# Elementwise work of stage 1 and of the weight conversions, done on VectorE instead of GpSimd

## The chip, the core and the metric

The kernel runs on one core of a Trainium2 chip. A core has five engines, each with an instruction queue of its own that is worked through in order: TensorE (PE, matrix products into PSUM), VectorE (DVE), ScalarE (ACT), GpSimd (POOL), and SyncE (SP), which here issues all DMAs. They wait for each other by semaphores. The metric is the device time of one execution in microseconds, lower is better; three executions of the kernel before gave 1600.19, 1600.63 and 1602.12.

## The reference

The attention is a double one: 32 "pack" vectors per head attend to the keys and values, and the queries attend to the result. Two feed-forward layers follow, each with its own nonlinearity.

```python
def _attn_ref(q, k, v, p):                     # 8 batches, 8 heads, 576 positions, 64 wide
    scale = 1.0 / np.sqrt(q.shape[-1])
    def sm_attn(qq, kk, vv):
        s = scale * np.matmul(qq, kk.transpose(0, 1, 3, 2))
        s = s - np.max(s, axis=-1, keepdims=True)
        a = np.exp(s)
        a = a / (np.sum(a, axis=-1, keepdims=True) + 1e-09)
        return np.matmul(a, vv)
    p_packed = sm_attn(p, k, v)                # 32 rows per head
    return sm_attn(q, p_packed, p_packed)

def _moe_ref(x, w_in, w_out):                  # 4608 tokens, 512 -> 2048 -> 512
    h = x @ w_in
    return (h - np.tanh(h)) @ w_out

def _moe2_ref(x, w_in, w_out):
    h = x @ w_in
    return (h * np.cos(h)) @ w_out
```

The weights arrive as 64-bit floats, seen by the kernel as pairs of 32-bit words.

## The kernel before

**Split numbers.** Products are wanted at float32 precision from matmuls on rounded operands (`F32R`). So an operand is kept as a high half (the value rounded by a ScalarE copy) and a low half (the value minus the high half), and a product is three matmuls: high by high, low by high, high by low. Making a low half is one elementwise subtraction: L359 for attention weights `a2`, L167 for weights `w1o`, `w2i`, `w2o`, L485 and L608 for the nonlinearities' results `gl`, L553 for the second layer's input `yhl`.

**Weight conversions (class `Conv`).** A tile of 128x512 64-bit weights (`st`) is loaded; then three parts, which the program places by tables. `a`: ScalarE scales the high words (L121). `b`: VectorE shifts the result left by 3 (L133, `shift`), merges the sign bit (L138, `sign`) and merges three bits from the low words (L143, `low`). `c`: ScalarE rounds the finished tile into the high half (L166) and the low half is subtracted (L167, on POOL). For 23 of the 32 tiles of the first layer (`POOL_SIGN`) the sign is done otherwise: ScalarE makes a tile of signs (L123), POOL multiplies by it (L148), and `sign` is left out. Tiles of `w1i` have no part `c`.

**Stage 1: attention and the first layer.** The tokens are 16 blocks of 288 (`blk`), two per batch. A step (128 in all, numbered n) takes two of the 16 slices of the hidden layer: `h1` multiplies the attention weights by `gw` (the packed values times `w_in`, made by `gmat`, split by `gsplit`), 12 matmuls; `el1` and `el2` compute h - tanh(h) with five VectorE instructions (L465 `t`, L466 `d`, L485 `gl` of the step before, L468 `y`, L472 copy_predicated into `y`); `ymm1`, 24 matmuls, follows two steps later. PSUM tiles for `h` and for all attention products share two buffers. The attention of batch b runs beside the steps of batch b-1 (functions put into `early[n]` and `mid[n]`): its second softmax is `s2m` (maximum, subtraction L336), `s2e`, `s2n` (sum, multiplication L348), `s2t`, `s2h` (split, L359). For b > 0 the three elementwise operations run on POOL; for b = 0 only the split does.

**What sets the order.** Everything ahead of step 15 is ordered by the scheduler of the kernel language, from then on the queues have the order in which the code issues. In a step the conversion's VectorE operations (`fill`) are put between the five instructions of `el2` by `interleave`. Steps 112 to 127 convert the second layer's weights, one tile per step; the rest is converted in `el_cos` of token block t = 0 of stage 2, three tiles per step.

**Stage 2: the second layer.** The tokens are nine blocks of 512 (t), with eight steps s each: `h2` (24 matmuls), `el_cos`, `ymm2` (24 matmuls) one step later. `el_cos` is a chain: ACT adds a constant (L586), DVE L589, ACT Sin and Square (L595, L596), DVE L599, ACT rounds `gh` (L605), DVE subtracts `gl` (L608). Between its links stand the calls `each("ca")` and `each("b")`, one conversion part each. The POOL split L553 of the next block's input stands in steps 2 to 5.

Of the kernel before, what the change touches and what calls it, by code (L numbers as in the profile page):

```python
# [10 lines left out]
F32 = mybir.dt.float32  # L11
# [4 lines left out]
AF = mybir.ActivationFunctionType  # L16
ALU = mybir.AluOpType
# [13 lines left out]
    "i2 i0 i3 i1 o1 o0 i4 i5 i6 i7 o3 o4 o2 o5 o7 i8 "  # L31
    "o6 i9 i10 i11 i14 o9 i12 i13 o8 i15 o11 o13 o12 o10 o15 o14"
).split()
POOL_SIGN = "11111111111111101011100010111000"
PRE_A = (0, 1, 1, 1, 1, 0, 1, 1, 1, 0, 1, 1, 0, 0, 0)
PRE_B = (1, 0, 1, 1, 2, 0, 2, 2, 0, 1, 2, 2, 0, 3, 0)
STEP_A = (1, 2, 2, 2, 1, 2, 1, 1, 1, 1, 0, 2, 1, 1, 1, 1, 1, 1, 0, 3, 1, 1)
# [13 lines left out]
def fused_kernel(ctx, tc, qT, kT, v, pT, w1i, w1o, w2i, w2o, ident, out):  # L51
    nc = tc.nc
    B, _, _, _, HB = qT.shape
# [13 lines left out]
    wp = ctx.enter_context(tc.tile_pool(name="wp", bufs=32))  # L67
# [7 lines left out]
    def f32(ap):  # L75
        return ap.bitcast(F32)

    def wtile(name):
        return wp.tile([128, 2, 512], F32R, tag="w", name=name)
# [7 lines left out]
    class Conv:  # L87
# [19 lines left out]
        def a(self):  # L107
            self.prefetch()
            if not self.ready:
                return  # L110
            kind, f, st = self.ready.pop(0)
            tmp, sgn = self.alloc_tmp(self.na, kind)
            self.na += 1
            w = tmp
            if kind == "w1i":
                if f // 2 not in w1in:
                    w1in[f // 2] = wp.tile([128, 2, 512], F32, tag="w", name="w1i")
                w = w1in[f // 2][:, f % 2, :]
            sv = st.rearrange("p (n two) -> p n two", two=2)
            hi, lo = sv[:, :, 1], sv[:, :, 0]  # L120
            nc.scalar.activation(out=w, in_=f32(hi), func=AF.Copy, scale=2.0 ** -112)  # L121
            if sgn is not None:
                nc.scalar.activation(out=sgn, in_=f32(hi), func=AF.Sign)  # L123
            self.done_a.append((kind, f, hi, lo, w, sgn))

        def b_ops(self):
            if not self.done_a:
                return []
            kind, f, hi, lo, w, sgn = self.done_a.pop(0)
            wi = w.bitcast(I32)  # L130

            def shift():
                nc.vector.tensor_scalar(  # L133
                    out=wi, in0=wi, scalar1=3, scalar2=None, op0=ALU.logical_shift_left
                )

            def sign():
                nc.vector.scalar_tensor_tensor(  # L138
                    out=wi, in0=hi, scalar=SGN, in1=wi, op0=ALU.bitwise_and, op1=ALU.bitwise_or
                )  # L140

            def low():
                nc.vector.scalar_tensor_tensor(  # L143
                    out=wi, in0=lo, scalar=29, in1=wi,
                    op0=ALU.logical_shift_right, op1=ALU.bitwise_or,
                )
                if sgn is not None:
                    nc.gpsimd.tensor_tensor(out=w, in0=w, in1=sgn, op=ALU.mult)  # L148
                if kind == "w1i":
                    self.bdone.add(f)  # L150
                else:
                    self.done_b.append((kind, f, w))
                self.prefetch()

            return [shift, low] if sgn is not None else [shift, sign, low]

        def b(self):
            for fn in self.b_ops():
                fn()

        def c(self):
            if not self.done_b:
                return
            kind, f, w = self.done_b.pop(0)
            t = wtile(kind)
            nc.scalar.activation(out=t[:, 0, :], in_=w, func=AF.Copy)  # L166
            nc.gpsimd.tensor_tensor(out=t[:, 1, :], in0=w, in1=f32(t[:, 0, :]), op=ALU.subtract)  # L167
            {"w1o": w1out, "w2i": w2in, "w2o": w2out}[kind][f] = t

        def c_all(self):  # L170
            while self.done_b:
                self.c()

        def need_i(self, f):
            while f not in self.bdone:
# [21 lines left out]
    def zip_ops(lists):  # L197
        out = []
        for i in range(0, len(lists), 2):
            pair = lists[i:i + 2]  # L200
            for j in range(max(len(p) for p in pair)):
                out += [p[j] for p in pair if j < len(p)]
        return out
# [51 lines left out]

    def attention(b, half, at=None, tsc=0, ttr=0, tpp=0, ts2=0):
        x = {}
        eng = nc.vector if b == 0 else nc.gpsimd

        def sc():  # L260
            k = ld.pop(("k", b, half))
# [71 lines left out]
        def s2m():  # L333
            m = att.tile([128, NG], F32, tag="m", name="m")
            nc.vector.tensor_reduce(out=m, in_=x["u3"], axis=AX.X, op=ALU.max)
            eng.tensor_tensor(  # L336
                out=x["u3"], in0=x["u3"], in1=m.to_broadcast([128, NG, 32]), op=ALU.subtract
            )

# [3 lines left out]
        def s2n():  # L343
            r = att.tile([128, NG], F32, tag="r", name="r")
            nc.vector.tensor_reduce(out=r, in_=x["u3"], axis=AX.X, op=ALU.add)
            nc.vector.tensor_scalar(out=r, in0=r, scalar1=1e-9, scalar2=None, op0=ALU.add)
            nc.vector.reciprocal(out=r, in_=r)
            eng.tensor_tensor(  # L348
                out=x["u3"], in0=x["u3"], in1=r.to_broadcast([128, NG, 32]), op=ALU.mult
            )  # L350

# [4 lines left out]
        def s2h():  # L356
            t = a2p.tile([128, 2, S], F32R, tag="a2", bufs=4, name="a2")
            nc.scalar.activation(out=t[:, 0, :], in_=x["ut"], func=AF.Copy)
            nc.gpsimd.tensor_tensor(  # L359
                out=t[:, 1, :], in0=x["ut"], in1=f32(t[:, 0, :]), op=ALU.subtract  # L360
            )
            a2[b, half] = t
# [66 lines left out]
    def h1(blk, s, st):  # L429
        b, j = divmod(blk, 2)  # L430
        h = pss("h")
        for x in range(2):
            f = 2 * s + x
            c0 = 128 * (f % 4)
            n = 0
            for ga, aa in ((0, 0), (1, 0), (0, 1)):
                for half in range(2):
                    nc.tensor.matmul(  # L438
                        out=h[:, x, 0:HB],
                        lhsT=gw[b, f // 4, half][:, ga, c0:c0 + 128],  # L440
                        rhs=a2[b, half][:, aa, HB * j:HB * j + HB],
                        start=(n == 0), stop=(n == 5),
                    )
                    n += 1
        st["h"] = h[:, :, 0:HB]
# [201 lines left out]
    def run_pool(name, **kw):  # L647
        c = tc.tile_pool(name=name, bufs=1, reuse_waits="tile", **kw)
        return c, c.__enter__()
# [14 lines left out]
        return wp.tile([128, 1024], I32, tag="w", name="st")  # L664

    def alloc_tmp(i, kind):
        t = wp.tile([128, 2, 512], F32, tag="w", name="wt")
        return t[:, 0, :], (t[:, 1, :] if POOL_SIGN[i] == "1" else None)

    conv = Conv([("w1" + o[0], int(o[1:])) for o in ORDER], 3, alloc_st, alloc_tmp)  # L670

# [100 lines left out]
    p2x = {}  # L772

    def open_p2r():
        attc.__exit__(None, None, None)
        cstc.__exit__(None, None, None)
        p2x["c"], p2x["r"] = run_pool("p2r", side="right")
        p2x["conv"] = Conv(
            todo2, 3,
            lambda i: p2x["r"].tile([128, 1024], I32, tag="st", bufs=3, name="st"),  # L780
            lambda i, kind: (p2x["r"].tile([128, 512], F32, tag="wt", bufs=2, name="wt"), None),
        )

    for n in range(-16, 0):
# [8 lines left out]
    for n, (blk, s) in enumerate(steps):  # L793
        if n == NSTEP * (NB - 2):
            open_p2r()
            p2r, conv2 = p2x["r"], p2x["conv"]
        if n == STEP_ORDERED:
            sched.__exit__(None, None, None)
            sched = tc.manual_schedule()
            sched.__enter__()  # L800
        st = {}
        h1(blk, s, st)
        el1(st)
        cv = conv2 if blk >= NB - 2 else conv
        cv.c_all()
        for fn in early[n]:
            fn()
        if hist:
            el3(hist[-1][2])
        if blk >= NB - 2:  # L810
            na = STEP_A2[n - NSTEP * (NB - 2)]
        else:
            na = STEP_A[n] if n < len(STEP_A) else 1
        fill = zip_ops([cv.b_ops() for _ in range(len(cv.done_a))])
        if n < 32:
            for _ in range(na):
                cv.a()
        el2(st, hist[-1][2] if hist else None, fill)
        if blk >= NB - 2:
            for _ in range(na):  # L820
                cv.a()
        if n == Y2LOAD:
            yr0 += [loady(0, k) for k in range(2)]
        if n == Y2SPLIT:
            yt = [splity(0, yr0.pop(0), nc.gpsimd) for k in range(2)]
            yr0 += [loady(0, k) for k in range(2, 4)]
        for fn in mid[n]:
            fn()
        hist.append((blk, s, st))
        if len(hist) == 3:  # L830
            hb, hs, hst = hist.pop(0)
            ymm1(hb, hs, hst)
            if hb < NP and hs == HS - 1:
                ypart1(hb)
            if hs == NSTEP - 1:
                yevac1(hb)
# [84 lines left out]
```

## Time and profile before

| | |
|---|---|
| median of 3 runs | 1600.63 us (1600.19 to 1602.12) |
| the profiled execution | 1600.74 us, its span 1599.0 us |
| PE busy | 1523.6 us, 95% |
| DVE busy | 1011.8 us, 63% |
| ACT busy | 871.4 us, 54% |
| POOL busy | 218.1 us, 14% |

The span is the time from the first to the last instruction of the profiled execution. Of POOL's time 60.1 us are the 34 splits L553, which the change leaves where they are. The engines' shares over the whole span say little here, as the program runs through stages with different loads: stage 1 ends at about 802 us, and beside its first 180 us and its last 90 us weights are converted. Rows of the trace give start and length of an instruction; a length in the order-of-time view runs until its end, and the next instruction of the same engine can start a little before.

### The profile page before, as it was taken

What the parts mean: (1) busy time and instruction counts of PE and PEld (TensorE: products, weight loads), DVE (VectorE), ACT (ScalarE), POOL (GpSimd) and SP (SyncE); (2) the same over time, 40 slices, a digit from 0 to 9 for tenths busy, and PEclk for the clock granted to TensorE, in tenths of its full rate; (3) what the DMA queues carried; (4) which work ended last, traced back from release to release, by engine and by line L of the source; (5) the groups of instructions that cost most, each with busy time, mean ns of one, the idle gap of its engine ahead of it and who ended that gap; (6) DMA issues with size and microseconds to landing.
All of it is one profiled execution on the core that took longest, in us unless ns stands there. A gap on an engine that the chain in (4) does not pass through costs nothing.

```text
span 1599.0 us, 25218 instructions
## 1 busy us (share of the span) xinstructions
PE 1523.6 (95%) x10336; PEld 1321.6 (83%) x10336; DVE 1011.8 (63%) x1357; ACT 871.4 (54%) x1331; POOL 218.1 (14%) x154
## 2 busy tenths in 40 slices
PE   3789999999999999997898999999999999999999
PEld 1678888999999999997877788888888888888887
DVE  6999888787878788789979433333333333333333
ACT  4768665665666566676666444444444443444443
POOL 3633110100101010111224010100001010101000
PEclk6799999999999999999999999999999999999999
DMA  9423222211211121022334101001010101010000
GB/s 347 147 100 119 78 79 90 64 46 34 76 36 58 60 64 60 31 80 95 94 114 139 40 14 40 14 1 53 0 47 7 42 12 40 14 40 14 23 4 27
DMA packets 49138, 97.63 MB, mean 61 GB/s; under 512 B 4928, under 2 KB 26432, under 8 KB 49024
## 3 DMA queue, kind: packets, MB, share of 16 engines
q1 hardware_dynamic: 49024, 96.03, 18.2%
q8 instruction: 81, 1.33, 0.4%
q14 instruction: 33, 0.27, 0.1%
HBM read 74.78 MB, written 21.23 MB: 60 GB/s over the span
## 4 chain that ended last, share of the span: by engine, by line
PE 78%; DVE 13%; issue 4%; ACT 2%; DMA 2%; SPq 0%; POOL 0%; DVEq 0%; ACTq 0%; POOLq 0%
PE y L625 22%; PE h L564 22%; PE y L500 20%; PE h L438 10%; DVE wt L133 2%; DVE y L468 2%; DVE wt L143 2%; PE gp L400 2%; DVE wt L138 2%; DVE d L466 1%; DVE t L465 1%; DVE y L472 1%; DVE gl L485 1%; ACT wt L121 1%; PE sc L250 1%
## 5 line engine op out<-in xcount | busy, mean ns | idle before, releaser
L564 PE MATMUL h<-yhl,w2i 128*128 128x512 f32 x1728 | 403.2, 389 | 0.0
L564 PEld LDWEIGHTS h<-yhl,w2i 128*128 128x128 f32 x1728 | 324.4, 188 | 67.1
L500 PE MATMUL y<-gh,w1o 128*128 128x288 f32 x2048 | 311.3, 304 | 16.8 <-ACT gh L480 11.8
L500 PEld LDWEIGHTS y<-gh,w1o 128*128 128x128 f32 x2048 | 284.1, 191 | 45.9 <-ACT t L453 14.9
L625 PE MATMUL y<-w2o,gh 128*128 128x512 f32 x1152 | 274.6, 390 | 7.4 <-ACT gh L605 7.4
L625 PEld LDWEIGHTS y<-w2o,gh 128*128 128x128 f32 x1152 | 215.7, 188 | 55.2 <-ACT gh L605 10.9
L589 DVE SCALAR_TENSOR_TENSOR a<-a,h 128x1024 f32<-128x1024 f32 (+1 forms) x74 | 88.0, 1192 | 244.9 <-ACT a L586 244.9
L438 PE MATMUL h<-a,g 128*128 128x288 f32 x1536 | 230.5, 300 | 12.8 <-ACT w1i L121 6.6
L438 PEld LDWEIGHTS h<-a,g 128*128 128x128 f32 x1536 | 214.9, 192 | 17.0 <-ACT w1i L121 7.5
L586 ACT ACTIVATE a<-h 128x1024 f32<-128x1024 f32 (+1 forms) x74 | 74.1, 1005 | 243.1 <-PE h L564 241.6
L453 ACT ACTIVATE t<-h 128x576 f32<-128x576 f32 x128 | 83.2, 650 | 207.6 <-PE h L438 207.3
L599 DVE SCALAR_TENSOR_TENSOR a<-a,h 128x1024 f32<-128x1024 f32 (+1 forms) x74 | 88.1, 1192 | 143.3 <-ACT a L596 143.3
L500 PE MATMUL y<-gl,w1o 128*128 128x288 f32 x1024 | 160.0, 299 | 1.2 <-DVE gl L485 1.2
L500 PEld LDWEIGHTS y<-gl,w1o 128*128 128x128 f32 x1024 | 145.0, 191 | 1.5 <-DVE gl L485 1.4
L625 PE MATMUL y<-w2o,gl 128*128 128x512 f32 x576 | 142.8, 390 | 0.0
L553 POOL TENSOR_TENSOR yhl<-yr,yhl 128x512 fp32r<-128x512 f32 x34 | 60.1, 1768 | 549.6 <-ACT yhl L552 549.6
L608 DVE TENSOR_TENSOR gl<-a,gh 128x1024 fp32r<-128x1024 f32 (+1 forms) x74 | 88.4, 1196 | 73.3 <-ACT gh L605 73.2
L465 DVE TENSOR_TENSOR t<-h,t 128x576 f32<-128x576 f32 x128 | 95.3, 744 | 52.8 <-ACT u L454 52.5
L625 PEld LDWEIGHTS y<-w2o,gl 128*128 128x128 f32 x576 | 108.2, 188 | 22.5 <-DVE gl L608 0.2
L472 DVE COPY_PREDICATED y<-k,t 128x576 f32<-128x576 int16 x128 | 118.4, 925 | 11.6
L595 ACT ACTIVATE a<-a 128x1024 f32<-128x1024 f32 (+1 forms) x74 | 76.7, 1037 | 83.3 <-DVE a L589 83.3
L605 ACT ACTIVATE gh<-a 128x1024 fp32r<-128x1024 f32 (+1 forms) x74 | 76.6, 1036 | 83.1 <-DVE a L599 83.1
(79 smaller groups left out, 1541.8 us busy)
## 6 DMA issues: line engine op xcount, KB each, us to landing
y<-ye SPq DMA_DIRECT2D x80, 144.0 KB, 1.9
yr<-y SPq DMA_DIRECT2D x36, 256.0 KB, 3.5
out<-o SPq DMA_DIRECT2D x36, 256.0 KB, 2.1
st<-w1i SPq DMA_DIRECT2D x16, 512.0 KB, 7.4
v<-vv SPq DMA_DIRECT2D x16, 512.0 KB, 4.5
st<-w1o SPq DMA_DIRECT2D x16, 512.0 KB, 6.5
st<-w2i SPq DMA_DIRECT2D x16, 512.0 KB, 3.6
st<-w2o SPq DMA_DIRECT2D x16, 512.0 KB, 3.6
```

What stands on the lines that cost most here:

```text
L438: nc.tensor.matmul(out=h[:, x, 0:HB], lhsT=gw[b, f // 4, half][:, ga, c0:c0 + 128], rhs=a2[b, half][:, aa, HB * j:HB * j + HB], start=(n = ...
L453: nc.scalar.activation(out=st["t"], in_=h, func=AF.Tanh)
L465: lambda: nc.vector.tensor_tensor(out=t, in0=hs, in1=t, op=ALU.subtract),
L472: lambda: nc.vector.copy_predicated(out=y, mask=k.bitcast(I16), data=t),
L500: nc.tensor.matmul(out=yps[blk][d][:, 0:HB], lhsT=w1out[f][:, wh, 128 * d:128 * d + 128], rhs=st[gg][:, x, :], start=(s in first and x == ...
L564: nc.tensor.matmul(out=h[:, x, :], lhsT=w2in[f][:, wa, 128 * k:128 * k + 128], rhs=yt[k][:, ya, :], start=(n == 0), stop=(n == 11),)
L589: nc.vector.scalar_tensor_tensor(out=a[:, x], in0=a[:, x], scalar=MAGIC, in1=h[:, x], op0=ALU.subtract, op1=ALU.subtract,)
L595: nc.scalar.activation(out=a[:, x], in_=a[:, x], func=AF.Sin, scale=PI)
L599: nc.vector.scalar_tensor_tensor(out=a[:, x], in0=a[:, x], scalar=1.0, in1=h[:, x], op0=ALU.subtract, op1=ALU.mult,)
L605: nc.scalar.activation(out=gh[:, x], in_=a[:, x], func=AF.Copy)
L608: nc.vector.tensor_tensor(out=gl[:, x], in0=a[:, x], in1=f32(gh[:, x]), op=ALU.subtract)
L625: nc.tensor.matmul(out=yps[t][m], lhsT=st[gg][:, x, 128 * m:128 * m + 128], rhs=w2out[f][:, wh, :], start=(s == 0 and x == 0 and part == 0 ...
```

## The change

The three attention operations (L336, L348, L359) go to VectorE for every batch. `POOL_SIGN` and its sign tiles go: all tiles take `shift`, `sign`, `low`, and the 23 ScalarE sign passes and 23 POOL multiplications are gone. The low half in `c` goes to VectorE. Called from a step of stage 1, `c_all` collects these subtractions and hands them back, and the step puts them at the head of `fill`, that is, between the instructions of `el2`. Called from `el_cos` or from `need`, `c` issues the subtraction at once.

```diff
-            tmp, sgn = self.alloc_tmp(self.na, kind)
+            tmp = self.alloc_tmp(self.na, kind)
...
             nc.scalar.activation(out=w, in_=f32(hi), func=AF.Copy, scale=2.0 ** -112)
-            if sgn is not None:
-                nc.scalar.activation(out=sgn, in_=f32(hi), func=AF.Sign)
...
-                if sgn is not None:
-                    nc.gpsimd.tensor_tensor(out=w, in0=w, in1=sgn, op=ALU.mult)
...
-            return [shift, low] if sgn is not None else [shift, sign, low]
+            return [shift, sign, low]
...
-        def c(self):
+        def c(self, later=None):
...
             nc.scalar.activation(out=t[:, 0, :], in_=w, func=AF.Copy)
-            nc.gpsimd.tensor_tensor(out=t[:, 1, :], in0=w, in1=f32(t[:, 0, :]), op=ALU.subtract)
+            rest = lambda: nc.vector.tensor_tensor(
+                out=t[:, 1, :], in0=w, in1=f32(t[:, 0, :]), op=ALU.subtract
+            )
+            rest() if later is None else later.append(rest)
...
         def c_all(self):
+            later = []
             while self.done_b:
-                self.c()
+                self.c(later)
+            return later
...
-        eng = nc.vector if b == 0 else nc.gpsimd
...
-            eng.tensor_tensor(
+            nc.vector.tensor_tensor(
                 out=x["u3"], in0=x["u3"], in1=m.to_broadcast([128, NG, 32]), op=ALU.subtract
...
-            eng.tensor_tensor(
+            nc.vector.tensor_tensor(
                 out=x["u3"], in0=x["u3"], in1=r.to_broadcast([128, NG, 32]), op=ALU.mult
...
-            nc.gpsimd.tensor_tensor(
+            nc.vector.tensor_tensor(
                 out=t[:, 1, :], in0=x["ut"], in1=f32(t[:, 0, :]), op=ALU.subtract
...
-        cv.c_all()
+        rest = cv.c_all()
...
-        fill = zip_ops([cv.b_ops() for _ in range(len(cv.done_a))])
+        fill = rest + zip_ops([cv.b_ops() for _ in range(len(cv.done_a))])
```

The new file is two lines shorter, so its line numbers are lower by one to five: L464 there is L465 here (`t`), L130 is L133 (`shift`), L135 is L138 (`sign`), L140 is L143 (`low`), L162 is L167 (the low half), L588, L598 and L607 are L589, L599 and L608.

First excerpt: VectorE's queue over one of the steps 114 to 125 of stage 1, before, from `t` to the copy_predicated.

```order
L465 TENSOR_TENSOR t<-h,t 128x576
L133 TENSOR_SCALAR wt<-wt 128x512
L466 TENSOR_TENSOR d<-u,h 128x576
L138 SCALAR_TENSOR_TENSOR wt<-st,wt 128x512
L485 TENSOR_TENSOR gl<-y,gh 128x576
L143 SCALAR_TENSOR_TENSOR wt<-st,wt 128x512
L468 SCALAR_TENSOR_TENSOR y<-y,d 128x576
L472 COPY_PREDICATED y<-k,t 128x576
```

The same engine and step in the changed kernel.

```order
L464 TENSOR_TENSOR t<-h,t 128x576
L162 TENSOR_TENSOR w2i<-wt,w2i 128x512
L465 TENSOR_TENSOR d<-u,h 128x576
L130 TENSOR_SCALAR wt<-wt 128x512
L484 TENSOR_TENSOR gl<-y,gh 128x576
L135 SCALAR_TENSOR_TENSOR wt<-st,wt 128x512
L467 SCALAR_TENSOR_TENSOR y<-y,d 128x576
L140 SCALAR_TENSOR_TENSOR wt<-st,wt 128x512
L471 COPY_PREDICATED y<-k,t 128x576
```

The low half (L162) stands second, and each conversion operation has moved one place down.

Second excerpt: VectorE's queue in `el_cos` of token block t = 0, before, from L589 to L599.

```order
L589 SCALAR_TENSOR_TENSOR a<-a,h 128x1024
L133 TENSOR_SCALAR wt<-wt 128x512
L138 SCALAR_TENSOR_TENSOR wt<-st,wt 128x512
L143 SCALAR_TENSOR_TENSOR wt<-st,wt 128x512
L599 SCALAR_TENSOR_TENSOR a<-a,h 128x1024
```

The same engine and place in the changed kernel.

```order
L588 SCALAR_TENSOR_TENSOR a<-a,h 128x1024
L130 TENSOR_SCALAR wt<-wt 128x512
L135 SCALAR_TENSOR_TENSOR wt<-st,wt 128x512
L140 SCALAR_TENSOR_TENSOR wt<-st,wt 128x512
L162 TENSOR_TENSOR w2i<-wt,w2i 128x512
L598 SCALAR_TENSOR_TENSOR a<-a,h 128x1024
```

The low half stands between the last conversion operation and the next link of the chain. ScalarE's queue keeps its order here: its copy for that low half (L166, L161 there) stands before the next tile's scaling.

## Rows read from the trace of the kernel before

**Rows 1.** The page's busy times: busy us (share of the span) xinstructions

```profile
PE 1523.6 (95%) x10336; PEld 1321.6 (83%) x10336; DVE 1011.8 (63%) x1357; ACT 871.4 (54%) x1331; POOL 218.1 (14%) x154
```

**Rows 2.** Busy us by stretch: length, PE, PEld, DVE, ACT, POOL, then clock, DMA share, GB/s

```profile
0.00:180.00 180.00, 136.13 (x1258) 111.34 (x1259) 163.59 (x251) 122.10 (x224) 69.59 (x52) 0.84 0.49 169
180.00:715.00 535.00, 527.78 (x5117) 491.04 (x5117) 440.63 (x705) 340.50 (x621) 46.28 (x37) 1.00 0.18 59
715.00:802.00 87.00, 74.00 (x512) 71.36 (x511) 82.41 (x106) 57.34 (x103) 19.38 (x14) 0.96 0.31 97
802.00:893.00 91.00, 83.61 (x361) 66.82 (x360) 76.72 (x82) 56.79 (x79) 32.02 (x23) 1.00 0.34 111
```

**Rows 3.** PE's waits, 20 to 180 us: total us, times, longest

```profile
PE gp L400 <- POOL w1i L148: 6.6, 2, 3.9
```

**Rows 4.** DVE by group, 260 to 300 us, where POOL is idle

```profile
L472 DVE COPY_PREDICATED y<-k,t 128x576 f32<-128x576 int16 x8 | 6.6, 822 | 0.8
...
L468 DVE SCALAR_TENSOR_TENSOR y<-y,d 128x576 f32<-128x576 f32 x7 | 5.2, 748 | 0.0
```

**Rows 5.** Instructions in order of time, 712 to 786 us: start us, us, engine

```profile
712.49 0.75 DVE L465 TENSOR_TENSOR t<-h,t 128x576 f32<-128x576 f32 x1
...
730.05 1.31 POOL L167 TENSOR_TENSOR w2o<-wt,w2o 128x512 fp32r<-128x512 f32 x1 [4.92 <-ACT w2o L166]
730.08 1.94 DVE L472 COPY_PREDICATED y<-k,t 128x576 f32<-128x576 int16 x1
...
732.58 0.41 DVE L133 TENSOR_SCALAR wt<-wt 128x512 int32<-128x512 int32 x1
...
785.07 1.78 DVE L143 SCALAR_TENSOR_TENSOR wt<-st,wt 128x512 int32<-128x512 int32 x1
```

**Rows 6.** Instructions in order of time, 808 to 886 us, token block t=0

```profile
808.45 1.29 DVE L589 SCALAR_TENSOR_TENSOR a<-a,h 128x512 f32<-128x512 f32 x2 [6.77 <-ACT a L586]
...
830.29 0.69 DVE L143 SCALAR_TENSOR_TENSOR wt<-st,wt 128x512 int32<-128x512 int32 x1
...
831.02 0.63 ACT L166 ACTIVATE w2i<-wt 128x512 fp32r<-128x512 f32 x1 [1.81 <-DVE wt L143]
...
832.15 1.06 ACT L595 ACTIVATE a<-a 128x1024 f32<-128x1024 f32 x1
...
833.24 1.06 ACT L596 ACTIVATE a<-a 128x1024 f32<-128x1024 f32 x1
...
884.98 1.21 DVE L599 SCALAR_TENSOR_TENSOR a<-a,h 128x1024 f32<-128x1024 f32 x1
```

**Rows 7.** Instructions in order of time, DVE, 790 to 802 us

```profile
790.30 0.74 DVE L465 TENSOR_TENSOR t<-h,t 128x576 f32<-128x576 f32 x1
...
790.97 0.74 DVE L466 TENSOR_TENSOR d<-u,h 128x576 f32<-128x576 f32 x1
...
793.86 0.75 DVE L465 TENSOR_TENSOR t<-h,t 128x576 f32<-128x576 f32 x1
...
800.39 1.29 DVE L553 TENSOR_TENSOR yhl<-yr,yhl 128x512 fp32r<-128x512 f32 x2 [1.28 <-ACT yhl L552]
```

**Rows 8.** DVE by group, 0 to 180 us: busy us, mean ns

```profile
L468 DVE SCALAR_TENSOR_TENSOR y<-y,d 128x576 f32<-128x576 f32 x20 | 19.4, 970 | 0.1
L472 DVE COPY_PREDICATED y<-k,t 128x576 f32<-128x576 int16 x19 | 17.5, 923 | 0.4
L485 DVE TENSOR_TENSOR gl<-y,gh 128x576 fp32r<-128x576 f32 x19 | 16.4, 863 | 0.0
L143 DVE SCALAR_TENSOR_TENSOR w1i<-st,w1i 128x512 int32<-128x512 int32 x16 | 15.4, 965 | 0.0
...
L143 DVE SCALAR_TENSOR_TENSOR wt<-st,wt 128x512 int32<-128x512 int32 x16 | 13.5, 850 | 0.0
L133 DVE TENSOR_SCALAR w1i<-w1i 128x512 int32<-128x512 int32 x16 | 12.3, 775 | 1.5 <-ACT w1i L121 1.5
L133 DVE TENSOR_SCALAR wt<-wt 128x512 int32<-128x512 int32 x16 | 11.5, 726 | 0.0
```

More of the change, by code (lines that the diff above doesn't have):

```diff
@@ L33 @@
 ).split()
-POOL_SIGN = "11111111111111101011100010111000"
 PRE_A = (0, 1, 1, 1, 1, 0, 1, 1, 1, 0, 1, 1, 0, 0, 0)
@@ L121, in a @@
             nc.scalar.activation(out=w, in_=f32(hi), func=AF.Copy, scale=2.0 ** -112)
-            if sgn is not None:
-                nc.scalar.activation(out=sgn, in_=f32(hi), func=AF.Sign)
-            self.done_a.append((kind, f, hi, lo, w, sgn))
+            self.done_a.append((kind, f, hi, lo, w))
         def b_ops(self):
@@ L128, in b_ops @@
                 return []
-            kind, f, hi, lo, w, sgn = self.done_a.pop(0)
+            kind, f, hi, lo, w = self.done_a.pop(0)
             wi = w.bitcast(I32)
@@ L666, in alloc_tmp @@
     def alloc_tmp(i, kind):
-        t = wp.tile([128, 2, 512], F32, tag="w", name="wt")
-        return t[:, 0, :], (t[:, 1, :] if POOL_SIGN[i] == "1" else None)
+        return wp.tile([128, 2, 512], F32, tag="w", name="wt")[:, 0, :]
     conv = Conv([("w1" + o[0], int(o[1:])) for o in ORDER], 3, alloc_st, alloc_tmp)
@@ L780, in open_p2r @@
             lambda i: p2x["r"].tile([128, 1024], I32, tag="st", bufs=3, name="st"),
-            lambda i, kind: (p2x["r"].tile([128, 512], F32, tag="wt", bufs=2, name="wt"), None),
+            lambda i, kind: (p2x["r"].tile([128, 512], F32, tag="wt", bufs=2, name="wt")),
         )
```

## The prediction

> **What bounds the kernel now.** I read the page's busy times first, then busy time by stretch, then PE's waits, then VectorE (DVE) by group and instruction by instruction. PE is busy 95% of the span, DVE 63%, POOL 14% [rows 1], but that mean hides four stages [rows 2]. From 0 to 180 us DVE works 163.6 of 180 and PE 136.1: DVE sets the pace. From 180 to 715 PE works 527.8 of 535 and DVE 440.6: PE sets it. From 715 to 802 (the last 13 steps of stage 1, with the second layer's weights converted beside them) DVE works 82.4 of 87 and PE 74.0: DVE again. From 802 to 893 (token block t=0 of stage 2, with 19 conversions left) PE works 83.6 of 91, DVE 76.7. After 893 PE is bound by itself and the change touches nothing there. PE waits for POOL itself only briefly: 6.6 us in two waits, for converted w1i halves [rows 3]. So the change is judged by DVE's time in three stretches, and by the order of its queue.
>
> **What POOL costs DVE today.** The same DVE instruction has two lengths. With POOL idle a copy_predicated takes 0.82 and a scalar_tensor_tensor L468 0.75 [rows 4]; a shift L133 takes 0.41 [rows 5]. With POOL busy, the copy_predicated that starts 0.03 behind a POOL instruction of 1.31 takes 1.94 [rows 5]: it stands until POOL is through. L143 takes 1.78 beside a POOL split [rows 5] and 0.69 without one [rows 6]. So taking work from POOL gives DVE something back, and the question is whether that pays for the work added.
>
> **0 to 180 us: +2.6.** Added to DVE: 23 sign merges, 16 low halves of w1o, and 8 attention instructions. A queued DVE instruction starts 0.07 before the one ahead of it ends (790.30 + 0.74 against 790.97 [rows 7]); two 128x512 subtractions took 1.29, the second adding 0.60 [rows 7]. So 23 x 0.61 + 16 x 0.60 + 8 x 0.67 = 14.0 + 9.6 + 5.3 = 28.9 (0.61 and 0.67 are 0.69 and 0.75 less the overlap). Given back, from the means of [rows 8] less the undisturbed lengths (0.75 for L468, taken for L485 too, 0.82 for L472, 0.69 for L143, 0.41 for L133): L468 20 x 0.22 = 4.4; L472 19 x 0.10 = 1.9; L485 19 x 0.11 = 2.1; L143 16 x 0.275 + 16 x 0.16 = 7.0; L133 16 x 0.365 + 16 x 0.316 = 10.9; sum 26.3. Since DVE is the bound, the difference of 2.6 is lost. ScalarE loses 23 Sign passes, but works 122 of 180 [rows 2] and sets nothing. This stretch is ordered by the scheduler, so its order changes everywhere. Bounds: if the order lets DVE stand for ScalarE's copy (0.63) before each of 16 low halves, +2.6 + 10.1 = +12.7; if the balance is zero and PE's waits for POOL go, -6.6. I take 2.6, the sum of the rows.
>
> **180 to 715 us: 0.** 36 attention instructions x 0.67 = 24 us go to DVE, which stands idle 94 of 535 [rows 2]; PE's work covers them, as DVE's results are used two steps later. Were the cover gone in the few steps where attention and the weight products meet, a third of it, +8, would show; none can be won, as PE is the bound. I take 0, by the idle time.
>
> **715 to 802 us: -6.4.** One conversion per step. The t subtraction of step 114 starts at 712.49, that of step 126 at 790.30 [rows 5, 7]: 77.8 for 12 steps, 6.48 each. After: the five main instructions take 793.86 - 790.30 = 3.56 [rows 7], shift, sign and low 0.34 + 0.61 + 0.61 = 1.56, the low half 0.60: 5.72. The low half stands second in the step's queue (first order excerpt); its ScalarE copy needs only the `low` of the step before, with copy_predicated and t in between (1.5), longer than the copy, so it should not wait. 12 x 5.72 = 68.6, plus POOL's two yhl splits that stay, 1.1 each by L143's 1.78 [rows 5], = 70.8. That is 7.0 less; the 13th low half, in step 126, takes 0.6 back. Bounds: PE's own step of 5.2 (36 matmuls at 74.0 us busy over 512 [rows 2]) would allow -15; a wait of 0.63 at each low half makes +1. I take the queue's sum.
>
> **802 to 893 us: +9.4.** Here the low half is not put between main instructions but right ahead of one (second order excerpt): the subtraction (L167 before, L162 now) directly before the main instructions L589, L599 and L608. DVE works in order, so L589 now stands behind a subtraction that waits for ScalarE's copy, and that copy waits for the conversion `low` just before it: L143 ends at 830.98, the copy starts at 831.02 [rows 6]. Before, POOL took this tail and DVE went on. One third of a step, from main instruction to main instruction: conversion 1.56, hop 0.04, copy 0.63, hop 0.04, subtraction 0.69, main 1.21 - 0.07 = 1.14: 4.10. The third that holds Sin and Square has these in the conversion's place: 0.03 + 2.15 (832.15 to 834.30) - 0.07, then the same: 4.61. From L589's end in step 0 (809.74) to L599's end in step 6 (886.19) the kernel before took 76.45 [rows 6]. After: 7 x 4.61 + 12 x 4.10 = 81.5, plus four POOL yhl splits (steps 2 to 5) x 1.1 = 4.4: 85.9, so +9.4. PE waits for gh of step 6 at the end of this, and nothing later makes it up. Bounds: with no wait for the copy 7 x 4.61 + 12 x 3.30 = 71.9, -4.6; with the ScalarE yhl split (about 0.6) also in line four times, +11.8. I take 9.4, since the order shows the wait and [rows 6] its links.
>
> **Sum.** 2.6 + 0 - 6.4 + 9.4 = +5.6, on the profiled execution's 1600.74 us (span 1599.0, the rest around it unchanged): 1606.3. The median of the three runs is 1600.63, so the same difference holds against it.
>
> **Rivals.**
> *A zero sum.* What DVE gains from POOL's silence it spends on POOL's work, in each stage. For it: 26.3 against 28.9 in the first stage. Against it: 1.1 for 0.6 per step after 715, and the queue wait after 802. It gives 0, or 1600.7. The Trainium skill (Perfetto Trace Analysis, Optimizing Scalar/DVE Operations) says this as a rule: the two engines share a read port into SBUF, so moving operations between them might not help. By that rule the time would be 1600.7 too; [rows 5] agree with the shared port, and [rows 6] are why I do not take the rule's sum.
> *Faster: POOL's delay was on the path.* In the first stage PE's products of weights wait for POOL's sign multiplication [rows 3]; without it the chain to the first steps is shorter, and DVE's new order fills the time. Price -6.6 in place of +2.6: -6.6 - 6.4 + 9.4 = -3.6, 1597.1. It decides when the first stage gains over 6.2. For it: POOL took 69.6 us for some 46 instructions there [rows 2], 1.5 each against 0.6. Against: DVE stays the bound there, and its load does not fall.
> *Much slower: PE waits in the long middle.* A third of the 24 us comes uncovered: +5.6 + 8 = +13.6, 1614.3. For it: PE and ScalarE meet DVE through two shared PSUM buffers. Against: 94 us idle.
>
> **How the numbers follow.** Forecast 0.52, zero sum 0.20, faster 0.14, much slower 0.14. The measurement tells no change from one under 0.2%, 3.2 us. Of the forecast's own range, 1602 to 1610, some 0.10 lies within that bound: slower 0.42 + 0.14 = 0.56, same 0.20 + 0.10 = 0.30, faster 0.14. The range reaches from the faster rival to just short of the much slower one: 1597 to 1613.
>
> **What would show it.** Right: copy_predicated at 0.82 in the steps after 715 and a step of 5.7; the steps of t=0 from L589 to L589 at 12.8 to 13.9 (three thirds, without and with 1.1) instead of 12.1 (76.45 over 19 thirds, times three), with DVE idle before the low half until ScalarE's copy ends; the t subtraction of step 114 within 4 us of 712.49. Wrong: L133 and L143 still long with POOL idle (then POOL was not the cause); no idle time before the subtractions after 802; PE idle between 180 and 715 grown by more than 3 us.

## The result and the profile after

The changed kernel takes 1617.81 us (median of 4 runs, 1616.52 to 1619.34) against 1600.41 (4 runs, 1599.73 to 1602.12): ratio 1.0107, 95% interval 1.009 to 1.0125. It is slower, as forecast, but by 17 us and not by 5.6; the time lies above the range.

The page's busy times of the changed kernel, answering to [rows 1]:

```profile
PE 1532.7 (95%) x10336; PEld 1325.4 (82%) x10336; DVE 1021.8 (63%) x1472; ACT 860.6 (53%) x1308; POOL 64.9 (4%) x39
```

DVE has 115 instructions more and only 10.0 us more work, so the amount of work alone does not explain the loss. By stretch (columns as in [rows 2], the bounds moved with the stages):

```profile
0.00:180.00 180.00, 138.02 (x1239) 111.37 (x1240) 158.75 (x291) 107.86 (x197) 0.30 (x5) 0.94 0.47 166
180.00:717.00 537.00, 520.42 (x5037) 481.04 (x5036) 453.47 (x732) 330.98 (x603) 0.00 (x0) 1.00 0.18 58
717.00:806.00 89.00, 83.89 (x604) 82.13 (x603) 84.64 (x134) 68.90 (x121) 5.90 (x2) 0.98 0.34 103
806.00:909.00 103.00, 87.66 (x366) 69.50 (x365) 76.48 (x103) 57.66 (x82) 7.44 (x4) 0.97 0.31 98
```

In the middle PE stands idle 16.6 of 537 where it was 7.2 of 535. The last stretch is 103 long for what took 91.

To place the loss I read four marks in both traces: the start of the `t` subtraction of step 25 and of step 112, the end of the first main instruction of t=0 (L589, L588 after), and the end of the span. After less before:

| stretch | forecast | measured |
|---|---|---|
| A, to step 25 | +2.6 | +3.7 |
| B, steps 25 to 112 | 0 | +11.5 |
| C1, step 112 to the first main instruction of t=0 | -6.4 | -10.1 |
| C2, from there on | +9.4 | +11.6 |
| sum | +5.6 | +16.6 |

**B.** PE's waits from 215 to 717 us (total us, times, longest):

```profile
PE h L437 <- DVE d L465: 8.8, 11, 1.3
```

The same view of before lists no wait of `h` for `d`. One of the eleven, in order of time:

```profile
426.60 0.78 DVE L353 STREAM_TRANSPOSE ut<-u 128x576 f32<-128x576 f32 x1
427.42 0.68 ACT L357 ACTIVATE a<-ut 128x576 fp32r<-128x576 f32 x1 [1.72 <-DVE ut L353]
...
428.13 0.76 DVE L358 TENSOR_TENSOR a<-ut,a 128x576 fp32r<-128x576 f32 x1 [0.75 <-ACT a L357]
...
428.81 0.75 DVE L464 TENSOR_TENSOR t<-h,t 128x576 f32<-128x576 f32 x1
...
429.48 0.74 DVE L465 TENSOR_TENSOR d<-u,h 128x576 f32<-128x576 f32 x1
...
430.37 1.83 PE L437 MATMUL h<-a,g 128*128 128x288 f32 x12 [1.25 <-DVE d L465]
```

Read it from the bottom: the next `h` needs a PSUM buffer that `d` frees; `d` stands behind `t`, and `t` behind the low half of attention, for which DVE stood idle 0.75 until ScalarE's copy came. POOL's queue took that wait before, and `t` went on; the same place in the trace of before:

```profile
417.17 0.78 DVE L354 STREAM_TRANSPOSE ut<-u 128x576 f32<-128x576 f32 x1
417.86 0.74 DVE L465 TENSOR_TENSOR t<-h,t 128x576 f32<-128x576 f32 x1
...
418.75 1.45 POOL L359 TENSOR_TENSOR a<-ut,a 128x576 fp32r<-128x576 f32 x1 [3.69 <-ACT a L358]
```

**C1.** One step of DVE in order of time, answering to [rows 5] and [rows 7]:

```profile
738.70 0.77 DVE L464 TENSOR_TENSOR t<-h,t 128x576 f32<-128x576 f32 x1
739.36 0.71 DVE L162 TENSOR_TENSOR w2i<-wt,w2i 128x512 fp32r<-128x512 f32 x1
739.96 0.77 DVE L465 TENSOR_TENSOR d<-u,h 128x576 f32<-128x576 f32 x1
740.63 0.45 DVE L130 TENSOR_SCALAR wt<-wt 128x512 int32<-128x512 int32 x1
740.96 0.78 DVE L484 TENSOR_TENSOR gl<-y,gh 128x576 fp32r<-128x576 f32 x1
741.63 0.71 DVE L135 SCALAR_TENSOR_TENSOR wt<-st,wt 128x512 int32<-128x512 int32 x1
742.23 0.78 DVE L467 SCALAR_TENSOR_TENSOR y<-y,d 128x576 f32<-128x576 f32 x1
742.90 0.71 DVE L140 SCALAR_TENSOR_TENSOR wt<-st,wt 128x512 int32<-128x512 int32 x1
743.50 0.84 DVE L471 COPY_PREDICATED y<-k,t 128x576 f32<-128x576 int16 x1
744.22 0.76 DVE L464 TENSOR_TENSOR t<-h,t 128x576 f32<-128x576 f32 x1
```

No idle time, no instruction stretched, and the step is 5.52, not 5.72.

**C2.** DVE in order of time in t=0, answering to [rows 6]:

```profile
831.24 1.21 DVE L598 SCALAR_TENSOR_TENSOR a<-a,h 128x1024 f32<-128x1024 f32 x1
832.37 0.42 DVE L130 TENSOR_SCALAR wt<-wt 128x512 int32<-128x512 int32 x1
832.82 0.69 DVE L135 SCALAR_TENSOR_TENSOR wt<-st,wt 128x512 int32<-128x512 int32 x1
833.55 0.69 DVE L140 SCALAR_TENSOR_TENSOR wt<-st,wt 128x512 int32<-128x512 int32 x1
834.94 0.69 DVE L162 TENSOR_TENSOR w2o<-wt,w2o 128x512 fp32r<-128x512 f32 x1 [0.70 <-ACT w2o L161]
835.55 1.22 DVE L607 TENSOR_TENSOR gl<-a,gh 128x1024 fp32r<-128x1024 f32 x1
```

A wait before the low half is there, as forecast, in every third: 0.70, and 0.95 where Sin and Square stand. The third is 4.31 here and 4.57 where Sin and Square stand; forecast were 4.10 and 4.61.

### The profile page after: what moved, and what is told of

Same layout as the page of the kernel before. It is cut to its first block, busy times and chain, and to the rows that moved or that the text cites. A ratio compares the mean times of both kernels' runs of the same rounds, so it can differ in the third digit from the quotient of the medians.

```text
span 1615.6 us, 25068 instructions
## 1 busy us (share of the span) xinstructions
PE 1532.7 (95%) x10336; PEld 1325.4 (82%) x10336; DVE 1021.8 (63%) x1472; ACT 860.6 (53%) x1308; POOL 64.9 (4%) x39
## 4 chain that ended last, share of the span: by engine, by line
PE 69%; DVE 21%; ACT 5%; issue 4%; DMA 1%; SPq 0%; DVEq 0%; ACTq 0%
PE y L624 22%; PE h L563 22%; PE y L499 14%; PE h L437 8%; DVE d L465 2%; DVE y L471 2%; DVE t L464 2%; DVE y L467 2%; DVE g L418 1%; DVE wt L135 1%; DVE gl L484 1%; DVE wt L130 1%; DVE wt L140 1%; PE gp L399 1%; ACT gh L479 1%
## 5 line engine op out<-in xcount | busy, mean ns | idle before, releaser
L624 PE MATMUL y<-w2o,gh 128*128 128x512 f32 x1152 | 277.9, 393 | 15.3 <-ACT gh L604 15.3
L588 DVE SCALAR_TENSOR_TENSOR a<-a,h 128x1024 f32<-128x1024 f32 (+1 forms) x74 | 88.0, 1192 | 244.9 <-ACT a L585 244.9
L585 ACT ACTIVATE a<-h 128x1024 f32<-128x1024 f32 (+1 forms) x74 | 74.2, 1005 | 249.5 <-PE h L563 241.7
L598 DVE SCALAR_TENSOR_TENSOR a<-a,h 128x1024 f32<-128x1024 f32 (+1 forms) x74 | 88.1, 1192 | 143.3 <-ACT a L595 143.3
L607 DVE TENSOR_TENSOR gl<-a,gh 128x1024 fp32r<-128x1024 f32 (+1 forms) x74 | 88.4, 1196 | 73.3 <-ACT gh L604 73.2
L464 DVE TENSOR_TENSOR t<-h,t 128x576 f32<-128x576 f32 x128 | 95.9, 749 | 47.3 <-ACT u L453 47.3
L604 ACT ACTIVATE gh<-a 128x1024 fp32r<-128x1024 f32 (+1 forms) x74 | 76.7, 1036 | 92.0 <-DVE a L598 92.0
L552 POOL TENSOR_TENSOR yhl<-yr,yhl 128x512 fp32r<-128x512 f32 x34 | 64.6, 1900 | 1435.7 <-ACT yhl L551 1435.7
L471 DVE COPY_PREDICATED y<-k,t 128x576 f32<-128x576 int16 x128 | 105.8, 827 | 10.3 <-DVE y L467 0.5
```

The source lines that it names most:

```text
L464: lambda: nc.vector.tensor_tensor(out=t, in0=hs, in1=t, op=ALU.subtract),
L471: lambda: nc.vector.copy_predicated(out=y, mask=k.bitcast(I16), data=t),
L588: nc.vector.scalar_tensor_tensor(out=a[:, x], in0=a[:, x], scalar=MAGIC, in1=h[:, x], op0=ALU.subtract, op1=ALU.subtract,)
L598: nc.vector.scalar_tensor_tensor(out=a[:, x], in0=a[:, x], scalar=1.0, in1=h[:, x], op0=ALU.subtract, op1=ALU.mult,)
L604: nc.scalar.activation(out=gh[:, x], in_=a[:, x], func=AF.Copy)
L607: nc.vector.tensor_tensor(out=gl[:, x], in0=a[:, x], in1=f32(gh[:, x]), op=ALU.subtract)
```

## The experiments

Each ran in 4 to 11 runs beside 15 to 20 of the kernel before, on the same chip; the median of before was 1600.6 to 1600.9 there. Stretches are read at the marks above, in one trace each, against the trace of before. The change and experiments 1, 2, 3 and 6 have the same order in their first steps and give +3.7 to +5.9 in A, so a difference of 2.2 in A is not read. In the other stretches some traces hold a stretch of about 3 us at a lower granted clock of TensorE, which can add 0.5 to 1.6; it is named where it matters.

**1. Low half of attention back on POOL** for batches 2 to 7, the rest as changed.

```diff
-            nc.vector.tensor_tensor(
+            (nc.gpsimd if b > 1 else nc.vector).tensor_tensor(
                 out=t[:, 1, :], in0=x["ut"], in1=f32(t[:, 0, :]), op=ALU.subtract
```

> The changed kernel, with only the attention split's low half (L358 there) back on POOL for batches 2 to 7; the softmax subtraction and multiplication stay on VectorE. In the changed kernel steps 25 to 112 lost 11.5 us. Theory (place in the queue): that low half stands ahead of the step's t and d and waits for ScalarE's copy, d then frees the PSUM buffer of the next h too late; without it 8 to 11 us come back, 1607 to 1610. Rival (load): VectorE simply has too much work there; a third of the added work goes, so about 4 us come back, 1614.

Measured: 1607.35 (1605.98 to 1610.32), ratio 1.0046 (1.0033 to 1.0058). B falls from +11.5 to +1.3, and PE's waits of `h` for `d` between 215 and 717 us are gone; what is left there:

```profile
PE y L499 <- DVE ye L529: 2.6, 1, 2.6
PE gp L399 <- DVE d L465: 1.8, 1, 1.8
```

The second line stands in the trace of before too. Of the +1.3 that is left, 1.4 comes in step 30, which takes 6.83 where before takes 5.47: behind PE's wait of 2.6 the granted clock is 0.50, the lower of its two levels (1.2 of 2.4 GHz), from 249.5 to 252.5 us. So the loss of the middle hangs on this one instruction of 0.75, twelve times in six batches. The other two attention instructions, as many and as long, stayed on DVE and cost nothing that shows.

**2. Low half on DVE, but at the end of its step** (behind copy_predicated).

```diff
             early[at + ts2 + 3].append(s2h)      # ScalarE's copy alone
+            mid[at + ts2 + 3].append(s2l)        # the subtraction, on DVE
```

> The changed kernel, with the attention split's low half of batches 2 to 7 still on VectorE but issued at the end of its step, behind copy_predicated, instead of ahead of t; the same work in another place. Place in the queue: 8 to 11 us come back, 1607 to 1610, and PE's waits for d (L465) in the middle of stage 1 go from about 9 us to under 2. Load: no change, 1617 to 1618.

Measured: 1611.63 (1610.97 to 1613.90), ratio 1.0068 (1.0055 to 1.0082), between the two expectations; B +5.8. PE now waits in another place:

```profile
PE gp L405 <- DVE d L471: 4.9, 6, 1.8
```

One of the six, of 1.8, stands in the trace of before too; the other five are new. DVE's order at such a place, with the low half (L364) and PE's product that waits:

```profile
422.47 0.75 DVE L364 TENSOR_TENSOR a<-ut,a 128x576 fp32r<-128x576 f32 x1
...
424.43 0.76 DVE L347 TENSOR_TENSOR u<-u,r 128x576 f32<-128x576 f32 x1
425.11 0.75 DVE L470 TENSOR_TENSOR t<-h,t 128x576 f32<-128x576 f32 x1
425.77 0.74 DVE L471 TENSOR_TENSOR d<-u,h 128x576 f32<-128x576 f32 x1
...
426.66 1.10 PE L405 MATMUL gp<-w1i,pt 64*32 64x256 f32 x32 [0.62 <-DVE d L471]
```

Without the wait for the copy the low half is still 0.67 more ahead of the next `d`, in a step already full of attention. How much each costs is read best from step 41 to step 105, four whole batches at a granted clock of 1.00 in all three traces: there the lag on before grows by 7.30 in the change and by 1.80 here, and falls by 0.95 in experiment 1. So of what the low half costs on DVE some two thirds come from its place ahead of `t`, with the wait, and one third from its length in the crowded step. B's +5.8 itself also holds some 1.8 from two stretches at the lower clock, in steps 25 and 30.

**3. Low half of t=0 behind the main instruction**, the rest as changed.

```diff
         each("ca")                    # the subtraction is kept back
         for x in parts:
             nc.vector.scalar_tensor_tensor(   # L598, likewise L588, L607
...
+        flush()                       # and issued here
         each("b")
```

> The changed kernel, with the weights' low half in el_cos issued behind the main VectorE instruction (L588, L598, L607) instead of ahead of it. Theory (wait): the main instruction no longer stands for ScalarE's copy; VectorE's work per step is 3 x 1.14 + 3 x 0.60 + 3 x 1.79 = 10.6, under PE's 10.9, so from L588 of step 0 to L598 of step 6 it takes 69 to 74 instead of 88.0 us: 1599 to 1604. Rival (load): the same number of VectorE instructions, the same time, 1616 to 1618.

Measured: 1600.78 (1598.91 to 1601.65), ratio 0.9998 (0.9989 to 1.0007): C2 falls from +11.6 to -6.1. The same stretch of DVE, in order of time:

```profile
828.89 0.68 DVE L162 TENSOR_TENSOR w2i<-wt,w2i 128x512 fp32r<-128x512 f32 x1
829.50 0.42 DVE L130 TENSOR_SCALAR wt<-wt 128x512 int32<-128x512 int32 x1
829.95 0.69 DVE L135 SCALAR_TENSOR_TENSOR wt<-st,wt 128x512 int32<-128x512 int32 x1
830.67 0.69 DVE L140 SCALAR_TENSOR_TENSOR wt<-st,wt 128x512 int32<-128x512 int32 x1
831.28 1.22 DVE L614 TENSOR_TENSOR gl<-a,gh 128x1024 fp32r<-128x1024 f32 x1
```

No wait: ScalarE's copy has the main instruction's 1.22 to finish in. The third is 3.52 (L604 starts at 827.76), and one swap of two instructions is worth 17.

**4. C1 alone**: the kernel before, with only the low halves of steps 112 to 127 on DVE, between `el2`'s instructions.

```diff
-            nc.gpsimd.tensor_tensor(out=t[:, 1, :], in0=w, in1=f32(t[:, 0, :]), op=ALU.subtract)
+            def rest(eng):
+                eng.tensor_tensor(out=t[:, 1, :], in0=w, in1=f32(t[:, 0, :]), op=ALU.subtract)
+            rest(nc.gpsimd) if later is None else later.append(lambda: rest(nc.vector))
...
-        cv.c_all()
+        rest = cv.c_all(blk >= NB - 2)       # put into fill, as in the change
```

> The kernel before, with one part of the change alone: the low halves of the second layer's weights that are made in steps 112 to 127 go to VectorE, between the instructions of el2; everything else stays on POOL. Theory (POOL blocks VectorE's copy_predicated): this stretch gains as in the changed kernel, 9 to 11 us, 1590 to 1592, with copy_predicated at 0.83. By the prediction's sum 6.4 us, 1594. Rival (zero sum): 1600.

Measured: 1590.84 (1589.81 to 1591.46), ratio 0.9939 (0.9927 to 0.9952). C1 -10.0, all else within 0.2. copy_predicated takes 0.83 on average in these steps, where it took 1.66 before.

**5. C1 and the later low half of t=0 together**, all else as before the change: the edits of 3 and 4.

> The kernel before with two of the change's four parts, each put where DVE does not wait: the low halves of steps 112 to 127 on DVE between el2's instructions, and the low halves of token block t=0 of stage 2 on DVE behind the main instruction instead of ahead of it. Signs, the first layer's low halves and attention stay on POOL. If the parts add, C1 gives -10.0 as in the run with that part alone, and what follows step 0 of t=0 gives -6.1 as in the run with the later low half, 0 elsewhere: 1600.8 - 16.1 = 1584.7, range 1583 to 1587. If the stretches lend each other time (the clock, or PE's queue running ahead), 1588 to 1592.

Measured: 1585.25 (1583.83 to 1586.34), ratio 0.9897 (0.9884 to 0.9911); C1 -10.1, C2 -6.0. The parts add.

**6. All three attention instructions back on POOL** for batches 2 to 7 (`eng = nc.vector if b < 2 else nc.gpsimd`), the rest as changed.

> The changed kernel with all three attention instructions of batches 2 to 7 back on POOL (subtraction of the maximum, multiplication by the reciprocal, low half); the low half alone back on POOL left steps 25 to 112 at +1.3. If those steps lose time only through DVE's attention work, they come to 0 (within 0.5) and the whole to 1606.0, range 1605 to 1607.5, 1.3 less than with the low half alone. If the remaining 1.3 is something else (the order left over from the first steps), the time stays at 1607.3.

Measured: 1609.82 (1607.96 to 1610.44), ratio 1.0049 (1.0036 to 1.0061); the time was missed, and most of the miss is the granted clock. Of B's +1.5, 1.3 comes in step 25. Its row (columns as in [rows 2]) in the trace of before, then here:

```profile
211.59:221.01 9.42, 7.85 (x93) 6.78 (x94) 9.22 (x18) 6.06 (x12) 1.29 (x2) 1.00 0.09 31
216.13:226.81 10.68, 9.12 (x91) 8.04 (x92) 9.40 (x19) 5.84 (x11) 1.35 (x2) 0.84 0.17 57
```

PE needs 1.27 more for the same products: behind a wait of 1.8 the clock was granted at 0.50 from 219.5 to 222.0 us. The same wait stands in the trace of before, where the clock stays at 1.00. Another 1.6 comes after step 6 of t=0, where this kernel is the changed one: PE had waited 3.1 for `gh`, the clock is 0.50 from 895.8 to 898.0 us, and the next products take 4.4, where the changed kernel at the same place has a clock of 1.00 and needs 3.0. Without the two, B is +0.2 and this execution would have taken some 1606.9 (1609.82 less 2.9, an estimate). So with all three instructions on POOL the middle loses nothing, and by experiment 1 the subtraction and the multiplication are free on DVE as well.

**7 to 10. The first stage, one part at a time.** Each is the kernel before with one edit: all signs on DVE (7), only the low halves of `w1o` on DVE (8, the edit of 4 with `blk < NB - 2`), one sign on DVE (9), all signs on POOL, the opposite way (10).

```diff
-POOL_SIGN = "11111111111111101011100010111000"
+POOL_SIGN = "00000000000000000000000000000000"   # 7
+POOL_SIGN = "11101111111111101011100010111000"   # 9
+POOL_SIGN = "11111111111111111111111111111111"   # 10
```

> The kernel before with only the sign merges moved: all 32 of the first layer's conversions merge the sign on DVE (23 more instructions there), the Sign passes of ScalarE and POOL's multiplications go. By the prediction's accounts 23 x 0.61 = 14.0 is added, and POOL's silence gives back its share by instructions, 23 of 47 of 26.3 = 12.9: +1.1, 1602, range 1600 to 1604, all of it before step 25. By the rival that POOL's delay was on PE's path (6.6 us of waits for converted w1i halves): -5, 1596. If DVE's added work counts in full, +14, 1615.

> The kernel before with only the 16 low halves of w1o moved from POOL to DVE, as in the change ahead of the step's own conversion instructions. By the prediction's accounts 16 x 0.60 = 9.6 is added and 16 of 47 of 26.3 = 9.0 given back: +0.6, 1601.4, range 1600 to 1603. If DVE stands for ScalarE's copy before each low half, as it does in attention and in stage 2: 16 x 0.63 = 10 more, 1611. If the first steps' loss of 3.7 to 5.9 in the changed kernel comes from this part, 1604 to 1607.

> The kernel before with one sign merge of 23 moved (the fourth conversion, w1i 3, merges its sign on DVE). If the first stage's loss of 4 to 6 in the runs so far is an amount of work, one instruction is worth 1/23 of the 5.2 that all 23 signs cost: 0.2, and the time stays at 1600.6 to 1601.2. If it is the new order that the scheduler makes of the first steps whenever a part is moved, one instruction can cost as much as 23: up to +5, in either direction, 1598 to 1606.

> The kernel before with the other 9 sign merges moved the opposite way, from DVE to POOL. If the first stage is set by the amount of work on DVE, this takes 9 x 0.61 = 5.5 off it and gives 9 delays by POOL (1.1 each where it meets a DVE instruction), -5 to +4 by a smooth account; moving signs to DVE cost +5.2 for 23, so the opposite would be -2.0 for 9: 1598.6. If any other order than the present one costs some 4, this is slower too, although the direction is opposite: 1603 to 1607.

| | moved | median us | ratio (95%) | A |
|---|---|---|---|---|
| 7 | 23 signs to DVE | 1604.97 | 1.0024 (1.0016 to 1.0033) | +5.2 |
| 8 | 16 low halves to DVE | 1605.00 | 1.0027 (1.0018 to 1.0036) | +4.4 |
| 9 | 1 sign to DVE | 1603.07 | 1.0013 (1.0004 to 1.0022) | +2.3 |
| 10 | 9 signs to POOL | 1604.54 | 1.0024 (1.0014 to 1.0033) | +4.7 |
| change | all to DVE | 1617.81 | 1.0107 (1.009 to 1.0125) | +3.7 |

The loss follows neither the amount nor the direction. The values of A are too close to be ranked, but all four medians lie above the kernel before, with intervals that leave out 1. (The trace of experiment 9 has another +1.5 in B, all of it in step 30, at a clock of 0.50 from 246.5 to 249.5 us: it belongs to that execution and not to the edit.) One window to the `t` of step 25 (columns as in [rows 2]) for before, the change, and experiment 10:

```profile
0.00:211.60 211.60, 166.72 (x1572) 139.05 (x1572) 188.09 (x291) 139.08 (x254) 70.63 (x53) 0.86 0.44 152
```

```profile
0.00:215.30 215.30, 171.39 (x1572) 141.65 (x1572) 187.68 (x338) 127.33 (x232) 0.30 (x5) 0.95 0.43 150
```

```profile
0.00:216.30 216.30, 167.88 (x1572) 140.37 (x1572) 190.72 (x281) 144.18 (x263) 85.46 (x62) 0.97 0.44 149
```

With 47 instructions more, DVE's busy time is 0.4 less: POOL's silence pays for them. Its idle time is what grows, 23.5 to 27.6. In experiment 10, with 10 instructions fewer, DVE is busy 2.6 longer beside the busier POOL, and idle 2.1 longer. The granted clock is not the cause, as its mean is 0.86 in the row of before and 0.95 and 0.97 in the slower two. What is left is the order that the scheduler makes of the first 15 steps; this is argued, as no run changes the order alone. With the change the `t` of step 0 comes 4.2 earlier than before and that of step 8 3.7 later; between the two DVE is idle 5.6 of 74.2 us, where it was 0.2 of 66.3. Every other order tried was 2 to 6 slower than the present one; which feature of it is good was not tried.

**11. Everything of attention on DVE, in a step with room**: experiment 5, and for batches 2 to 7 all three instructions on DVE, the two low halves in step at + 14, behind `gl` and `y`.

```diff
+            room[at + 14].append(s2l)
...
-        fill = rest + zip_ops([cv.b_ops() for _ in range(len(cv.done_a))])
+        fill = [str, str] * bool(room[n]) + room[n] + rest + zip_ops(...)   # str: an empty place
```

> The kernel with the two parts of the run c1 and cos (1585.25), and in addition all three attention instructions of batches 2 to 7 on DVE, but the two low halves of a batch issued in a later step, at + 14 (before at + 11 and at + 13), behind gl and behind y of that step, where the traces show 3.9 us of DVE work in 4.8 to 5.2. If the middle's loss was the place in the queue and the crowded steps, steps 25 to 112 lose at most 1 and the time is 1585.3 to 1586.3. If DVE's added load costs wherever it stands, as 3.6 of it did with the low half at the end of its own step, +3.6: 1589. If it is as in the changed kernel, +9.2: 1594.5.

Measured: 1584.91 (1584.47 to 1585.06), ratio 0.9900 (0.9887 to 0.9914); B -0.7 and A +1.1, so nothing beside experiment 5. PE's busy time between 180 and 703 us, PE being idle 6.6 and POOL all the time:

```profile
180.00:703.00 523.00, 516.38 (x5034) 479.60 (x5033) 450.30 (x727) 330.14 (x603) 0.00 (x0) 1.00 0.18 59
```

The step at + 14 of one batch, DVE in order of time:

```profile
425.52 0.75 DVE L477 TENSOR_TENSOR d<-u,h 128x576 f32<-128x576 f32 x1
426.18 0.76 DVE L496 TENSOR_TENSOR gl<-y,gh 128x576 fp32r<-128x576 f32 x1
426.85 0.76 DVE L370 TENSOR_TENSOR a<-ut,a 128x576 fp32r<-128x576 f32 x1
427.52 0.75 DVE L479 SCALAR_TENSOR_TENSOR y<-y,d 128x576 f32<-128x576 f32 x1
```

In the changed kernel B lost 11.5 with these 24 us of work on DVE; here they cost nothing: the same instructions of batches 2 to 7 on the same engine, and only the low half at another place.

## Why the prediction went wrong

**The step that failed is "180 to 715 us: 0".** Its ground, "PE's work covers them, as DVE's results are used two steps later", holds for `gl` and `y`, not for `t` and `d`: these free the PSUM buffer of `h`, and with two buffers shared with attention the next product but one needs it. DVE's 94 us of idle time were real but a mean over steps; the step with the low half has none beside the wait itself. The rival *much slower* named the two PSUM buffers and gave 1614.3, with the bound +8 for this stretch; measured was +11.5, of which experiment 1 removes 10.2; what is left there is the clock's 1.4 of step 30. I did not read the order of the low half against `t` as I had read it in t=0, though it was the same trap: a subtraction in an in-order queue that waits for ScalarE's copy.

**"802 to 893 us: +9.4"** was right in mechanism (experiment 3: +11.6 becomes -6.1) and small by 2.2. The term mis-sized is the conversion of 1.56: `shift`, `sign` and `low` rework one tile, each starts only when the one ahead has ended (832.37, 832.82, 833.55, end 834.24), and together they take 1.87. Of the 0.31 more, 0.10 comes back, mostly since the low half overlaps the main instruction by 0.08: 12 thirds times 0.21 are 2.5, less 7 times 0.04. I had added up lengths less an overlap of 0.07 that neighbours have only when neither needs the other.

**"715 to 802 us: -6.4"** was right in mechanism (experiment 4, -10.0 alone) and too small, for the same reason turned round. The five main instructions' 3.56 held the wait of copy_predicated for `y`; a conversion instruction between them fills it, so the step is 5.52, and 12 x 0.20 = 2.4 more is won. Another 2.2 was put down for POOL's two `yhl` splits, which began only 2.9 before the twelve steps ended and delayed none of them (12 x 5.52 = 66.2 from `t` to `t`, forecast 70.8). Of this 4.6, some 0.9 came back before the first main instruction of t=0 (+1.5 where 0.6 was put down).

**"0 to 180 us: +2.6"** is near in size (+3.7) and wrong in its ground: DVE's balance was -0.4, not +2.6, and the loss is idle time, by what is left that of a new order. That the size came near is luck: the same order gave 3.7 to 5.9. What POOL's silence gives back showed as forecast. DVE by group, 0 to 180 us, answering to [rows 8]:

```profile
L471 DVE COPY_PREDICATED y<-k,t 128x576 f32<-128x576 int16 x19 | 15.6, 821 | 0.0
L467 DVE SCALAR_TENSOR_TENSOR y<-y,d 128x576 f32<-128x576 f32 x19 | 14.3, 750 | 0.0
...
L140 DVE SCALAR_TENSOR_TENSOR w1i<-st,w1i 128x512 int32<-128x512 int32 x16 | 10.8, 684 | 0.0
...
L130 DVE TENSOR_SCALAR w1i<-w1i 128x512 int32<-128x512 int32 x16 | 6.7, 416 | 1.5 <-ACT w1i L120 1.5
```

**The rivals.** *Faster* falls: PE's 6.6 of waits for POOL [rows 3] do go, and the first stage is later all the same (experiment 7, +5.2). *A zero sum*, the rule of the Trainium skill (Perfetto Trace Analysis, Optimizing Scalar/DVE Operations) that work moved between the two engines might not help, holds for DVE's busy time in the first stage (188.1 and 187.7) and not for the time: the same kind of move is worth -10.0 in experiment 4, +11.6 in the change's t=0 and -6.1 there in experiment 3. Of the signs named ahead, the short copy_predicated (0.85 in the steps after 727, 1.66 before), the short L130 and L140 and the idle time before the low halves of t=0 were right; the step named as 5.7 was 5.52, and the steps of t=0, named as 12.8 and 13.9, were 13.2 and 14.3; the `t` of step 114 came at 727.7, 15.2 late, and PE's idle time in the middle grew by 9.4 where 3 was the limit: those two point at B.

## What to carry over

Before an instruction is moved into another engine's in-order queue, write down what it waits for and what stands behind it: here 19 subtractions of 0.7, each waiting for another engine's copy, cost 11.6 us ahead of the main instructions and gained 6.1 behind them. Judge cover by the step, not by the mean idle time, and by the first thing that the queue releases (here a PSUM buffer), not by the last result. Where a scheduler orders a stretch, a small edit anywhere in it brings a new order, worth 2 to 6 us here whatever the edit was. And before a difference of 1 to 2 us in a single trace is given a cause, read the granted clock of that stretch in windows of a few us: here it was the cause in six places.

## What the runs showed of the hardware

Dependent DVE instructions don't overlap: in t=0 `low` begins 0.73 after `sign`, which takes 0.69 and whose result it needs, whereas in C1 an instruction of 0.71 is followed after 0.60 by one that does not need it (742.90 to 743.50). So work that is independent, put between two dependent instructions, costs less than its length: a step of C1 took in four conversion instructions and got to 5.52, under the 5.72 of the sum.

TensorE's granted clock fell to 0.50 for about 3 us in some executions and not in others of the same instructions. PE waits 1.8 us for the same product near step 25 in every trace; the clock falls behind that wait in experiments 2 and 6 only. Step 25 took 9.42 at a clock of 1.00 and 10.68 at a mean of 0.84.
